# Normalising a key tile ahead of or behind the next tile's evictions, in a fused linear attention and expert kernel

## The chip, the cores and the metric

The kernel runs on one core of a Trainium2 chip. The core has five engines that matter here, each with its own queue of instructions: PE (TensorE, matrix products, with PEld for its weight loads), DVE (VectorE), ACT (ScalarE), POOL (GpSimd) and SP (SyncE, which issues DMAs). The metric is the device time of one execution in microseconds (us). Before the change it is 776.78 us, the median of three runs from 776.26 to 778.11.

## The reference

For 2048 tokens of width 448 a gate mixes two results, `g * a + (1 - g) * b`. `a` is a linear attention with 16 heads of 28 columns, `b` a mixture of 8 experts of which every token uses two. The part that matters here is the feature map of the keys and the state that is summed from it:

```python
pk = jnp.einsum("bhsd,hdf->bhsf", k, w_phi)
phi_k = jnp.concatenate([_softmax(pk, axis=-1), _softmax(-pk, axis=-1)], axis=-1)
kv = jnp.einsum("bhsf,bhsd->bhfd", phi_k, v)
z  = jnp.einsum("bhsf->bhf", phi_k)
num = jnp.einsum("bhqf,bhfd->bhqd", phi_q, kv)
den = jnp.einsum("bhqf,bhf->bhq", phi_q, z)[..., None] + 1e-6
```

The experts of each token come from its two highest logits `xf @ w_gate`, with a softmax over the two as their weights:

```python
topk_idx = jnp.argsort(-logits, axis=-1)[:, :K]
gates = _softmax(topk_val, axis=-1)
for e in range(E):
    w = (gates * (topk_idx == e)).sum(-1, keepdims=True)
    out = out + w * (_silu(xf @ w1[e]) @ w2[e])
```

## The kernel before

The 2048 tokens are cut into 16 tiles of 128 rows (`NT`). Every product is made of three parts, since each operand is split into a rounded part and a rest. The program has three stages: a pass over the key tiles, which sums the state of the attention (about 21 to 111 us of the profile), a pass over the query tiles (to about 215 us), and the experts (the rest).

The pass over the key tiles is the loop at L689. Step t does the following:

- `advance(STEPS[t])` (L692) takes the next piece of `route`, a generator with the routing of 8 tiles: small DVE instructions on 128x64 or 128x8 elements (L436 to L492). `STEPS` gives one piece to each of the steps 9 to 14 and none to step 15.
- `lower` (L694), in steps 10 to 12, takes the maxima of a query tile on DVE (L603) and subtracts them on POOL (L608).
- `norm(t - 1)` (L696) normalises the predecessor's features `ek[t - 1]`: DVE sums them by head and sign (L632) and takes the reciprocals (L633, into `sk`), and POOL multiplies 128x896 features by them (L634). In step 15 it stands behind `key(t)` (L701).
- `key(t)` (L699): 11 matmuls make `pk` in a bank of PSUM (L149); DVE takes each head's maximum and minimum (L625, twice) and evicts the two differences into `ek[t]` in SBUF (L626, L627).
- Behind them come a value tile or a query tile's products on PE (L664), ACT's exponential of `ek[t]` in place (L714), and `store` (L720), which issues indirect DMAs with routing records from POOL (L497).
- `state(t)` (L639) adds a normalised tile to the state on PE (L643). From step 8 on it is called in pairs: step 10 sums tiles 7 and 8, step 12 tiles 9 and 10, step 14 tiles 11 and 12, each pair behind the products of its step. Tiles 13, 14 and 15 follow after the loop (L757, L758, L762), between products of the first query tiles and transposes of `flip` (L745).

The order of the instructions on PE, ACT and DVE is the order in which they are written (`manual_schedule`, L352), and POOL's large instructions and its stores are tied to each other by `in_turn`. `pk` has two banks, so the products of tile t wait until DVE has evicted tile t - 2.

Of the kernel before, what the change touches and what calls it, by code (L numbers as in the profile page):

```python
# [25 lines left out]
NT = S // P  # L26
# [57 lines left out]
KLATE = 7  # L84
# [10 lines left out]
def gated_mix(ctx: ExitStack, tc: tile.TileContext, xt, xq, wk, wq, wv, wphi, wo, w12, out):  # L95
# [39 lines left out]
    def in_turn(i, kind=None):  # L135
        if runs["on"]:
            if kind is None or kind != runs["kind"]:
                runs.update(before=runs["last"], last=[], kind=kind)
            for o in runs["before"]:
                follow(i, o)  # L140
            runs["last"].append(i)
        return i
# [52 lines left out]
    def load_in_turn(dst, src):  # L195
        i = nc.sync.dma_start(dst, src)
        if loads:
            follow(i, loads[-1])
        loads.append(i)
        return i  # L200
# [50 lines left out]
    for what in LANDING:  # L251
        t = int(what[1])
# [52 lines left out]
    def xsplits(t):  # L305
        xsplit(XH[t], XL[t], xr[t], nc.gpsimd if t in XLP else nc.vector)
        if t + 3 < NT:
            xload(t + 3)
# [4 lines left out]
    def fold(n, c):  # L313
        f = [bank("O", f"wf{n}{c}{a}")[:, 0:D].rearrange("p (c g f) -> p c g f", c=2, g=4) for a in range(2)]
        for i in range(2):
            for g in range(4):
                for a, k in enumerate(half):
                    for b in half:
                        nc.tensor.matmul(f[a][b, i, g], raw[n][k, c + i, g * P + b.start:g * P + b.stop], bd[k, g],
                                         start=True, stop=True)  # L320
        for a in range(2):
            split(*(w[n][:, c:c + 2].rearrange("p c (g a f) -> p a c g f", g=4, a=2)[:, a] for w in (WH, WL)), f[a])
# [19 lines left out]
    def value(t):  # L342
        pv = bank("O", f"pv{t}")
        mm3(pv[:, 0:VG], kpairs(XH[t], XL[t], WH["v"], WL["v"]))
        value_out(t, pv)
# [149 lines left out]
    def store(n, behind=()):  # L495
        for at, what in stores[:n]:
            i = in_turn(nc.gpsimd.indirect_dma_start(  # L497
                out=tabd[:, :], out_offset=bass.IndirectOffsetOnAxis(ap=at, axis=0), in_=what, in_offset=None), "slots")
            after(i, [*filled, *behind])
            for o in sc:  # L500
                tc.declare_no_dep(i.ins, o.ins, reason="slots of their own")
            sc.append(i)
        del stores[:n]
# [91 lines left out]
    def signs(e, src):  # L595
        e4 = signed(e)
        nc.scalar.activation(e4[:, :, 0], src, AF.Copy)
        nc.scalar.activation(e4[:, :, 1], src, AF.Copy, scale=-1.0)
# [12 lines left out]
    def lower(e, n, pool):  # L611
        drop(e, tops(e, n, pool))


    def key(t):
        pk = bank("A", f"pk{t}")
        mm3(pk[:, 0:D], (kpairs if t else as_they_come)(XH[t], XL[t], WH["k"], WL["k"]))
        p = by_head(pk[:, 0:D])

        ek[t] = (pb.tile([P, 4, 512], F32, tag="wraw", name=f"ek{t}").rearrange("p c n -> p (c n)")[:, 0:2 * D]  # L620
                 if t >= KLATE and t % 2 else pb.tile([P, 2 * D], F32, tag="e", name=f"ek{t}", bufs=KLAG + 1))
        e4 = halves(ek[t])
        mx = [pb.tile([P, H], F32, tag=f"mk{i}", name=f"mk{i}_{t}") for i in range(2)]
        for m, op in zip(mx, (ALU.max, ALU.min)):
            nc.vector.tensor_reduce(out=m, in_=p, axis=AX.X, op=op)  # L625
        nc.vector.tensor_tensor(out=e4[:, :, 0], in0=p, in1=mx[0].unsqueeze(2).to_broadcast(b16), op=ALU.subtract)  # L626
        nc.vector.tensor_tensor(out=e4[:, :, 1], in0=mx[1].unsqueeze(2).to_broadcast(b16), in1=p, op=ALU.subtract)  # L627

    def norm(t):
        e = ek[t]  # L630
        s_ = pb.tile([P, 2 * H], F32, tag="s", name=f"sk{t}")
        nc.vector.tensor_reduce(out=s_, in_=by_head(e), axis=AX.X, op=ALU.add)  # L632
        nc.vector.reciprocal(s_, s_)  # L633
        in_turn(nc.gpsimd.tensor_tensor(out=by_head(e), in0=by_head(e), in1=s_.unsqueeze(2).to_broadcast([P, 2 * H, DH]),  # L634
                                        op=ALU.mult))
# [3 lines left out]
    def state(t):  # L639
        for g in range(4):  # L640
            for i in range(4):
                h = 8 * (g // 2) + 2 * i + g % 2
                nc.tensor.matmul(kvp[32 * i:32 * i + 32, g * 56:(g + 1) * 56], vbuf[t % len(vbuf)][:, h, :],  # L643
                                 ek[t][:, h * 56:(h + 1) * 56], start=t == 0 and g == 0, stop=t == NT - 1,
                                 skip_group_check=True)
# [3 lines left out]
    def advance(n):  # L649
        for _ in range(n):  # L650
            if routes and next(routes[0], 0) == 0:
                del routes[0]
# [4 lines left out]
    def ask(t, b=None, some=(0, 11)):  # L657
        if some[0] == 0:
            b = bank("A", f"pq{t}") if b is None else b
            pq[t] = by_head(b[:, 0:D])  # L660
            EQ[t] = ebuf[t % QBUFS]
        for k, (x, w) in enumerate(kpairs(XH[t], XL[t], WH["q"], WL["q"])):
            if some[0] <= k < some[1]:
                nc.tensor.matmul(pq[t].rearrange("p h d -> p (h d)"), x, w, start=k == 0, stop=k == 10)  # L664

    def raise_(t):
        nc.scalar.activation(EQ[t][:, :, 0:56], EQ[t][:, :, 0:56], AF.Exp)
# [21 lines left out]
    for t in range(NT):  # L689
        u = t + VAHEAD  # L690
        q = ASKS.get(t)
        advance(STEPS[t])  # L692
        if t - QWAIT in ASKS and ASKS[t - QWAIT] < QEARLY:
            lower(EQ[ASKS[t - QWAIT]], f"q{ASKS[t - QWAIT]}", pr)  # L694
        if 1 <= t < NT - 1:
            norm(t - 1)  # L696
        for v in SPLITS.get(t, ()):
            xsplits(v)
        key(t)  # L699
        if t == NT - 1:  # L700
            norm(t - 1)  # L701
        if u < NT:
            value(u)
        if q is not None:
            ask(q, early[:, q % 2 * 512:q % 2 * 512 + 512])
            signs(EQ[q], pq[q])
        if t in (2, 4):
            fold("q", t - 2)
        if 1 <= t < 5:
            c = t - 1  # L710
            nc.scalar.activation(WH["o"][:, c], raw["o"][:, c], AF.Copy)
            in_turn(nc.gpsimd.tensor_tensor(out=WL["o"][:, c], in0=raw["o"][:, c], in1=WH["o"][:, c].bitcast(F32),
                                            op=ALU.subtract))
        nc.scalar.activation(ek[t], ek[t], AF.Exp)  # L714
        if t - QWAIT in ASKS and ASKS[t - QWAIT] < QEARLY:
            raise_(ASKS[t - QWAIT])
        if t == 8:
            for r in range((NOUT - S) // P):
                rows_done.append(load_in_turn(out[S + r * P:S + (r + 1) * P, :], zero[:, 0:D]))
        store(KSTORES.get(t, 2))  # L720
        if KLAG <= t <= KLATE + 1:
            state(t - KLAG)
        elif t > KLATE and (t - KLATE) % 2:
            state(t - KLAG - 1)
            state(t - KLAG)
        if u + 1 in GROUPS:
            routes.append(route(GROUPS.index(u + 1) - 1))
# [796 lines left out]
```

## Time and profile before

| | us |
|---|---|
| median of three runs | 776.78 |
| lowest, highest | 776.26, 778.11 |
| profiled execution | 776.68 |
| its span, first to last instruction | 775.0 |
| outside the span | 1.68 |
| PE busy in the span | 764.5 |
| DVE busy in the span | 470.1 |
| POOL busy in the span | 343.9 |

The page shows one execution; its times count from the start of the span. An engine's busy time is the sum of its instructions. In a timeline each row gives an instruction's start, its duration, engine, line, operation, and what it writes and reads; a bracket at the end gives the idle time just before it and what ended that. A row with "x2" merges two of a kind. Instructions of DVE and ACT overlap a little with the next, so that a row can start before the end of the one above it.

### The profile page before, as it was taken

The numbers are of one execution on the slowest core, as the hardware profiler recorded it, in microseconds if no ns is written. First come the engines' busy times: TensorE is split into PE (matmuls) and PEld (weight loads), VectorE is DVE, ScalarE is ACT, GpSimd is POOL, SyncE is SP. The second block draws the span as 40 slices with busy tenths as digits, with TensorE's granted clock in tenths as the row PEclk, the third lists the DMA queues.
The fourth block names the chain that finished last, engine by engine and source line by source line (L and its number), as shares of the span: only waits on it lengthen the run. The fifth ranks groups of instructions, "written<-read, shape, count | busy, mean of one in ns | idle before, by whom it ended". The sixth has DMA issues, their size and how long they took to land. (4 is left out here: it accounts for less than half of the span.)

```text
span 775.0 us, 21224 instructions
## 1 busy us (share of the span) xinstructions
PE 764.5 (99%) x8890; PEld 714.3 (92%) x8890; DVE 470.1 (61%) x954; ACT 304.9 (39%) x522; POOL 343.9 (44%) x321
## 2 busy tenths in 40 slices
PE   9999999999999999999999999999999999999996
PEld 7888888888899999998999899999998999999996
DVE  4698978768766755565457345554654555465442
ACT  5543456567433333333334323332432333243220
POOL 4667877886224305521472337054234405423102
PEclk9999999999999999999999999999999999999999
DMA  8420000156344327433643454363345336434502
GB/s 277 131 88 1 2 2 27 39 114 209 114 155 123 128 102 154 134 106 95 147 142 124 90 149 151 111 157 132 127 114 157 128 111 160 137 125 112 168 2 48
DMA packets 42759, 88.95 MB, mean 115 GB/s; under 512 B 11438, under 2 KB 23126, under 8 KB 42660
## 3 DMA queue, kind: packets, MB, share of 16 engines
q1 hardware_dynamic: 32324, 70.24, 27.5%
q0 software_dynamic: 10192, 17.08, 11.3%
q8 instruction: 71, 1.16, 0.6%
q10 hardware_dynamic: 144, 0.23, 0.1%
q14 instruction: 28, 0.23, 0.1%
HBM read 73.53 MB, written 14.00 MB: 113 GB/s over the span
## 5 line engine op out<-in xcount | busy, mean ns | idle before, releaser
L1130 PE MATMUL acc<-w2h,hx 64*128 64x448 f32 (+3 forms) x1756 | 293.4, 362 | 0.0
L1071 PE MATMUL hp<-xgh,w1h 64*128 64x272 f32 (+4 forms) x1078 | 218.3, 331 | 0.9 <-SPq L1048 0.8
L1071 PE MATMUL hp<-xgh,w1l 64*128 64x272 f32 (+4 forms) x1078 | 217.7, 331 | 0.0
L1071 PE MATMUL hp<-xgl,w1h 64*128 64x272 f32 (+4 forms) x1078 | 217.5, 330 | 0.0
L1130 PEld LDWEIGHTS acc<-w2h,hx 64*128 64x128 f32 (+3 forms) x1756 | 200.1, 182 | 4.9 <-issue 1.0
L1104 DVE CAST hx<-hs 128x504 fp32r<-128x504 f32 (+5 forms) x154 | 55.3, 359 | 231.5 <-ACT hs L1098 231.4
L1130 PE MATMUL acc<-w2l,hx 64*128 64x448 f32 (+4 forms) x892 | 195.1, 362 | 0.0
L1098 ACT ACTIVATE hs<-hp 128x272 f32<-128x272 f32 (+4 forms) x154 | 66.3, 482 | 313.4 <-issue 216.7
L847 POOL DMA_INDIRECT xg<-in_xq_dram,idq x114 | 128.9, 1131 | 131.9 <-PE hp L1071 65.6
L1071 PEld LDWEIGHTS hp<-xgh,w1h 64*128 64x128 f32 x1078 | 145.3, 184 | 5.8 <-SPq L1048 1.2
L1071 PEld LDWEIGHTS hp<-xgl,w1h 64*128 64x128 f32 x1078 | 143.9, 184 | 4.0
L1071 PEld LDWEIGHTS hp<-xgh,w1l 64*128 64x128 f32 x1078 | 143.7, 184 | 3.1
L1023 POOL DMA_INDIRECT out_dram<-y,tabm x30 | 48.6, 1620 | 195.8 <-DVE y L1221 189.1
L1130 PEld LDWEIGHTS acc<-w2l,hx 64*128 64x128 f32 (+4 forms) x892 | 110.6, 182 | 2.2
L1107 DVE TENSOR_TENSOR hx<-hs,hx 128x504 fp32r<-128x504 f32 (+6 forms) x168 | 85.0, 513 | 5.3
L816 DVE TENSOR_TENSOR w1l<-wr,w1h 128x1024 fp32r<-128x1024 f32 x56 | 67.7, 1210 | 2.2 <-ACT w1h L814 2.1
L814 ACT ACTIVATE w1h<-wr 128x1024 fp32r<-128x1024 f32 x56 | 59.3, 1058 | 4.8 <-DMA wr<-in_w_dram 4.8
L816 DVE TENSOR_TENSOR w2l<-wr,w2h 128x896 fp32r<-128x896 f32 x46 | 49.5, 1076 | 0.0
L814 ACT ACTIVATE w2h<-wr 128x896 fp32r<-128x896 f32 x46 | 43.9, 954 | 0.0
L497 POOL DMA_INDIRECT tabd<-rec,slot_i x32 | 31.5, 984 | 10.1 <-issue 8.1
L634 POOL TENSOR_TENSOR ek<-ek,sk 128x896 f32<-128x896 f32 x16 | 27.2, 1700 | 16.8 <-DVE sk L633 10.3
L867 ACT ACTIVATE xgh<-xgt 128x512 fp32r<-128x512 f32 (+4 forms) x30 | 18.1, 605 | 39.5 <-DVE xgt L875 39.5
(242 smaller groups left out, 1004.1 us busy)
## 6 DMA issues: line engine op xcount, KB each, us to landing
wr<-in_w_dram SPq DMA_DIRECT2D x56, 512.0 KB, 3.7
wr<-in_w_dram SPq DMA_DIRECT2D x46, 448.0 KB, 4.3
kept<-in_w_dram SPq DMA_DIRECT2D x10, 448.0 KB, 5.5
out_dram<-aos SPq DMA_DIRECT2D x16, 224.0 KB, 2.6
xr<-in_xt_dram SPq DMA_DIRECT2D x10, 256.0 KB, 4.0
xg<-in_xq_dram,idq POOLq DMA_INDIRECT x114, 3.3
xr<-in_xt_dram SPq DMA_DIRECT2D x6, 192.0 KB, 3.9
out_dram<-zero SPq DMA_DIRECT2D x5, 224.0 KB
```

What stands on the lines that cost most here:

```text
L497: i = in_turn(nc.gpsimd.indirect_dma_start(out=tabd[:, :], out_offset=bass.IndirectOffsetOnAxis(ap=at, axis=0), in_=what, in_offset=None), ...
L634: in_turn(nc.gpsimd.tensor_tensor(out=by_head(e), in0=by_head(e), in1=s_.unsqueeze(2).to_broadcast([P, 2 * H, DH]), op=ALU.mult))
L814: nc.scalar.activation(h, raws[s][layer - 1], AF.Copy)
L816: nc.vector.tensor_tensor(out=l, in0=raws[s][layer - 1], in1=h.bitcast(F32), op=ALU.subtract)
L847: i = nc.gpsimd.indirect_dma_start(out=t[:, b], out_offset=None, in_=xq, in_offset=bass.IndirectOffsetOnAxis(ap=idq[:, e, 4 * c + b:4 * c ...
L867: nc.scalar.activation(xh, src, AF.Copy)
L1023: return nc.gpsimd.indirect_dma_start(out=out, out_offset=bass.IndirectOffsetOnAxis(ap=idx_ap, axis=0), in_=y, in_offset=None, compute_op= ...
L1071: meet(("first", i), a, lambda: nc.tensor.matmul(o[i], l, r, start=n == 0, stop=n == len(rounds) - 1), n == 0)
L1098: nc.scalar.activation(hs[:, tsl], hp, AF.Silu)
L1104: nc.vector.tensor_copy(h[:, tsl], hs[:, tsl])
L1107: nc.vector.tensor_tensor(out=h[:, a + o:b + o], in0=hs[:, a:b], in1=h[:, a:b].bitcast(F32), op=ALU.subtract)
L1130: meet((e, c), a, lambda: nc.tensor.matmul(acc[e][c][:l.shape[1], 0:D], l[half[a]], r[half[a]], start=new, stop=ends and c not in of[k + 1 ...
```

## The change

The bound between the two places of `norm(t - 1)` moves from step 15 to step 10. In the steps 10 to 14 the predecessor was normalised ahead of `key(t)`, and is now normalised behind it, as in step 15 before and after. `KLATE` is 7.

```diff
         advance(STEPS[t])
         if t - QWAIT in ASKS and ASKS[t - QWAIT] < QEARLY:
             lower(EQ[ASKS[t - QWAIT]], f"q{ASKS[t - QWAIT]}", pr)
-        if 1 <= t < NT - 1:
+        if 1 <= t < KLATE + 3:
             norm(t - 1)
         for v in SPLITS.get(t, ()):
             xsplits(v)
         key(t)
-        if t == NT - 1:
+        if t >= KLATE + 3:
             norm(t - 1)
         if u < NT:
             value(u)
```

On DVE, from the queue of step 10 into step 11, stood before (`sk` the sums and their reciprocals, `mk` maxima and minima, `pk` the products in PSUM, `mxq` a query tile's maxima, `f`, `sel` and `l` parts of the routing):

```order
L632 TENSOR_REDUCE sk_1179<-ek_1126 128x32
L633 RECIPROCAL sk_1179<-sk_1179 128x32
L625 TENSOR_REDUCE mk_10_1196<-pk_1183 128x16
L625 TENSOR_REDUCE mk_10_1197<-pk_1183 128x16
L626 TENSOR_TENSOR ek_1195<-pk_1183,mk_10_1196 128x16x28
L627 TENSOR_TENSOR ek_1195<-mk_10_1197,pk_1183 128x16x28
L440 TENSOR_REDUCE f_1172<-t_1171 128x8
L441 TENSOR_TENSOR sel_1166<-down,f_1172 128x64
L451 SCALAR_TENSOR_TENSOR l_1168<-sel_1166,L 128x64
L603 TENSOR_REDUCE mxq_1253<-eq_205 128x32
```

and now:

```order
L625 TENSOR_REDUCE mk_10_1192<-pk_1179 128x16
L625 TENSOR_REDUCE mk_10_1193<-pk_1179 128x16
L626 TENSOR_TENSOR ek_1191<-pk_1179,mk_10_1192 128x16x28
L627 TENSOR_TENSOR ek_1191<-mk_10_1193,pk_1179 128x16x28
L632 TENSOR_REDUCE sk_1198<-ek_1126 128x32
L633 RECIPROCAL sk_1198<-sk_1198 128x32
L440 TENSOR_REDUCE f_1172<-t_1171 128x8
L441 TENSOR_TENSOR sel_1166<-down,f_1172 128x64
L451 SCALAR_TENSOR_TENSOR l_1168<-sel_1166,L 128x64
L603 TENSOR_REDUCE mxq_1253<-eq_205 128x32
```

The sum and the reciprocal of tile 9 moved behind the four evictions of tile 10, and so directly ahead of the routing piece of step 11.

Further on, from step 13 into step 14, stood before on DVE (`gt` and `omg` are the gate and one minus the gate, 8 tiles at a time):

```order
L632 TENSOR_REDUCE sk_1379<-ek_1319 128x32
L633 RECIPROCAL sk_1379<-sk_1379 128x32
L625 TENSOR_REDUCE mk_13_1396<-pk_1383 128x16
L625 TENSOR_REDUCE mk_13_1397<-pk_1383 128x16
L626 TENSOR_TENSOR ek_1395<-pk_1383,mk_13_1396 128x16x28
L627 TENSOR_TENSOR ek_1395<-mk_13_1397,pk_1383 128x16x28
L459 TENSOR_SCALAR gt<-gt 128x8
L460 RECIPROCAL gt<-gt 128x8
L461 TENSOR_SCALAR omg_1163<-gt 128x8
```

and now:

```order
L625 TENSOR_REDUCE mk_13_1392<-pk_1379 128x16
L625 TENSOR_REDUCE mk_13_1393<-pk_1379 128x16
L626 TENSOR_TENSOR ek_1391<-pk_1379,mk_13_1392 128x16x28
L627 TENSOR_TENSOR ek_1391<-mk_13_1393,pk_1379 128x16x28
L632 TENSOR_REDUCE sk_1398<-ek_1315 128x32
L633 RECIPROCAL sk_1398<-sk_1398 128x32
L459 TENSOR_SCALAR gt<-gt 128x8
L460 RECIPROCAL gt<-gt 128x8
L461 TENSOR_SCALAR omg_1163<-gt 128x8
```

Here too the pair moved from ahead of the evictions to the place directly ahead of the routing piece. No instruction is added or removed; on PE, ACT, POOL and SP the sequence of operations is the same as before.

## Rows read from the trace of the kernel before

**Rows 1.** The page's part 1: busy time, share of the span and number of instructions of each engine.

```profile
PE 764.5 (99%) x8890; PEld 714.3 (92%) x8890; DVE 470.1 (61%) x954; ACT 304.9 (39%) x522; POOL 343.9 (44%) x321
```

**Rows 2.** Busy time by stretch, one answer each for 74 to 112 us and for 112 us to the end: the length of the stretch, then busy us (and instructions) of PE, PEld, DVE, ACT, POOL, the granted TensorE clock, the DMA share, GB/s.

```profile
74.00:112.00 38.00, 37.34 (x455) 32.86 (x454) 32.84 (x67) 18.66 (x33) 30.56 (x24) 1.00 0.02 2
...
112.00:775.00 663.00, 654.80 (x7660) 619.90 (x7658) 382.88 (x771) 251.04 (x412) 268.00 (x221) 1.00 0.42 120
```

**Rows 3.** Who waited for whom, PE over the whole span: us in total, times, longest.

```profile
PE warm L246 <- DVE blank L244: 1.1, 1, 1.1
PE hp L1071 <- SPq L1048: 0.8, 1, 0.8
PE et L745 <- ACT et L746: 0.7, 1, 0.7
PE n L936 <- DVE w L952: 0.6, 2, 0.3
PE ot L969 <- POOL om L957: 0.5, 1, 0.5
```

**Rows 4.** Timeline of all engines around the start of step 11.

```profile
81.98 1.71 POOL L634 TENSOR_TENSOR ek<-ek,sk 128x896 f32<-128x896 f32 x1
...
83.04 0.21 DVE L440 TENSOR_REDUCE f<-t 128x8 f32<-128x64 f32 x1
...
83.29 0.50 DVE L441 TENSOR_TENSOR sel<-down,f 128x64 f32<-128x64 f32 x1
...
83.82 0.29 DVE L451 SCALAR_TENSOR_TENSOR l<-sel,L 128x64 f32<-128x64 f32 x1
```

**Rows 5.** Timeline of DVE from step 12 to the start of step 15.

```profile
88.47 0.22 DVE L436 TENSOR_REDUCE m<-l 128x8 f32<-128x64 f32 x1
88.72 0.25 DVE L437 TENSOR_TENSOR t<-l,m 128x64 f32<-128x64 f32 x1
89.00 0.23 DVE L438 TENSOR_TENSOR t<-t,down 128x64 f32<-128x64 f32 x1
...
91.25 0.35 DVE L633 RECIPROCAL sk<-sk 128x32 f32<-128x32 f32 x1
91.52 1.08 DVE L625 TENSOR_REDUCE mk<-pk 128x16 f32<-128x448 f32 x2
...
93.58 0.21 DVE L440 TENSOR_REDUCE f<-t 128x8 f32<-128x64 f32 x1
...
94.04 0.06 DVE L454 MEMSET selb<- 128x4 uint32 x1
...
94.75 1.09 DVE L632 TENSOR_REDUCE sk<-ek 128x32 f32<-128x896 f32 x1 [0.33 <-ACT ek L714]
95.88 0.35 DVE L633 RECIPROCAL sk<-sk 128x32 f32<-128x32 f32 x1
...
98.21 0.17 DVE L459 TENSOR_SCALAR gt<-gt 128x8 f32<-128x8 f32 x1
...
98.64 0.17 DVE L461 TENSOR_SCALAR omg<-gt 128x8 f32<-128x8 f32 x1
99.44 1.09 DVE L632 TENSOR_REDUCE sk<-ek 128x32 f32<-128x896 f32 x1 [0.62 <-ACT ek L714]
...
102.89 1.15 DVE L625 TENSOR_REDUCE mk<-pk 128x16 f32<-128x448 f32 x2
...
106.13 0.35 DVE L633 RECIPROCAL sk<-sk 128x32 f32<-128x32 f32 x1
```

**Rows 6.** Timeline of POOL from step 13 to the end of the key tiles: the multiplications of tiles 12, 13, and (merged) 14 and 15, and two stores.

```profile
96.39 1.70 POOL L634 TENSOR_TENSOR ek<-ek,sk 128x896 f32<-128x896 f32 x1 [1.55 <-DVE sk L633]
...
101.09 1.70 POOL L634 TENSOR_TENSOR ek<-ek,sk 128x896 f32<-128x896 f32 x1 [0.57 <-DVE sk L633]
102.94 1.00 POOL L497 DMA_INDIRECT tabd<-rec,slot_i  x1 [0.16 <-issue]
104.25 0.98 POOL L497 DMA_INDIRECT tabd<-rec,slot_i  x1 [0.30 <-issue]
106.64 3.36 POOL L634 TENSOR_TENSOR ek<-ek,sk 128x896 f32<-128x896 f32 x2 [1.41 <-DVE kvs L750]
```

**Rows 7.** Timeline of DVE at three earlier or later places where the routing's instructions ran while POOL worked.

```profile
34.95 1.07 DVE L438 TENSOR_TENSOR t<-t,down 128x64 f32<-128x64 f32 x1
...
53.63 0.83 DVE L461 TENSOR_SCALAR omg<-gt 128x8 f32<-128x8 f32 x1
...
122.31 1.11 DVE L490 TENSOR_TENSOR s<-sel,slot 128x64 f32<-128x64 f32 x1
...
123.71 0.23 DVE L490 TENSOR_TENSOR s<-sel,slot 128x64 f32<-128x64 f32 x1
```

**Rows 8.** Timeline of POOL at the same three places.

```profile
34.79 1.15 POOL L712 TENSOR_TENSOR WLo<-wraw_o,WHo 128x448 fp32r<-128x448 f32 x1
...
53.29 1.14 POOL L712 TENSOR_TENSOR WLo<-wraw_o,WHo 128x448 fp32r<-128x448 f32 x1
...
121.64 1.70 POOL L608 TENSOR_TENSOR eq<-eq,mxq 128x896 f32<-128x896 f32 x1
```

**Rows 9.** Timeline of the weight loads at the two ends of the state's sum that the change reaches: the state of tiles 11 and 12, and of tile 15.

```profile
98.93 0.94 PEld L643 LDWEIGHTS kv<-ek,v 128*32 128x32 f32 x64 [0.31 <-issue]
...
110.05 0.45 PEld L643 LDWEIGHTS kv<-ek,v 128*32 128x32 f32 x32 [0.32 <-POOL ek L634]
```

## The prediction, written before the result was known

> **What bounds the kernel now.** I read the page's busy times first. PE is busy for 764.5 us of 775.0 [rows 1], so any time PE loses is lost for good, and what another engine saves is worth nothing unless PE waited for it. Next come the busy times by stretch, since the change lies in one of them: from 74 to 112 us PE is busy for 37.34 of 38.00 us, but DVE for 32.84 and POOL for 30.56 [rows 2]. In this stretch the two are close behind PE, unlike in the rest. Then PE's waits: none is over 1.1 us, and between 74 and 112 us there is one of 0.7 us, at a transpose [rows 3]. The one edge through which the normalisation ends the stretch is the state of tile 15: its first weight load, at 110.05 us, was released by POOL's multiplication [rows 9], which ends at 106.64 + 3.36 = 110.00 [rows 6]. So the key pass ends on the chain from DVE to POOL to PE, and it has no room there.
>
> Last, the timelines of DVE and POOL side by side, for who runs at the same time as whom. This decides the forecast. A routing instruction on DVE that reads two operands from SBUF takes about 0.25 us (L437 and L438 in step 12) [rows 5]. While a POOL multiplication or subtraction runs, the same kind takes until that has ended: L438 from 34.95 to 36.02, beside a POOL instruction that ends at 34.79 + 1.15 = 35.94; L461 to 54.46 beside one to 54.43; L490 to 123.42, 1.11 us, beside POOL's L608 to 123.34, and 0.23 us right after with POOL free [rows 7, 8]. Once the normalising multiplication does it too: L441 takes 0.50 us and ends at 83.79, 0.10 behind POOL's L634 [rows 4]. The evictions, with one operand in PSUM, are not held: those of tile 13 take 2.06 us from 96.15 to 98.21, like those of tile 12 [rows 5], with a multiplication beside them from 96.39 to 98.09 [rows 6].
>
> The Trainium skill has this as a rule: in "SBUF — State Buffer", section "Who interferes with whom", a VectorE instruction with two SBUF inputs contends with a GpSimd instruction that reads SBUF, and the port they share goes to one of them for a whole instruction. The trace agrees, with the 1.07, 0.83 and 1.11 us above. By the rule alone the change would be slower as well, by as many blocks.
>
> **The change, part by part.** Nothing is added or removed. In steps 10 to 14 the sum and the reciprocal go behind the evictions, which take 2.06 us from start to start (91.52 to 93.58) [rows 5]. Take r, the start of the reciprocal. POOL's multiplication starts at r + 0.51 (95.88 to 96.39) [rows 5, 6] and runs for 1.70, to r + 2.21; DVE's next instruction starts at r + 0.27 (91.25 to 91.52).
>
> Before, that next work was the evictions, with one operand in PSUM, and the routing piece followed at r + 0.27 + 2.06 = r + 2.33, when the multiplication was over. That is a fit to a tenth of a microsecond. After, the routing piece of the next step starts at r + 0.27, and the whole multiplication stands against it; the piece's blocked instruction ends near r + 2.30.
>
> - Step 11: r is 82.77, since step 11 still starts at 83.04. L441 then ends at 85.07 and L451 starts at 85.10 where it started at 83.82 [rows 4]: 1.28 us.
> - Step 12: L438 started 0.53 us into the step (89.00 - 88.47) and now starts at r + 2.33, which is 2.06 into it: 1.53 us.
> - Step 13: L454, behind L441, started 0.46 into the step (94.04 - 93.58) and now 1.98: 1.52 us.
> - Step 14: L461 ended 0.60 into the step (98.64 + 0.17 - 98.21) and now ends with the multiplication, 1.97 into it: 1.37 us.
>
> The sum is 5.70 us on DVE. Who comes first in steps 11 to 13 is open, as L441 or L437 would start at r + 0.52 and POOL at r + 0.51. It matters little: if DVE wins, POOL starts 0.26 later, and the next two-operand instruction of the piece (L451, L438, L455) is held instead. Only if POOL let the whole piece pass would a step cost nothing. So a block is bounded by 0 and 1.8 us, and I take the values above, since every overlap in rows 4, 7 and 8 shows DVE held.
>
> What goes away: DVE's two waits for the exponential, 0.33 us in step 13 and 0.62 in step 14 [rows 5], because a tile's sum now comes one key tile later. DVE is then 5.70 - 0.95 = 4.75 us late at the evictions of tile 15, which start at 102.89 + 4.75 = 107.64.
>
> On POOL a moved normalisation also moves its multiplication, past no other instruction, but later against the clock. Tile 13's reciprocal now stands directly ahead of tile 15's evictions, r = 107.37, so its multiplication starts at 107.88. The two stores of step 14 lie behind it in POOL's queue: 1.85 us from the multiplication's start to the first, 1.31 to the second, 1.0 for that one [rows 6]. So tile 14 starts at 112.04. Its reciprocal, at 106.13 + 4.75 = 110.88, would have allowed 111.39: the queue adds 0.65. Tiles 14 and 15 take 3.36 together, to 115.40, and the state of tile 15 starts at 115.45 where it started at 110.05: 5.4 us.
>
> On PE the wait shows up first at the state of tile 12, in step 14. Step 14 starts at 98.21 + 1.28 + 1.53 + 1.52 - 0.33 = 102.21, so tile 12 is multiplied from 102.45 to 104.15. PE would be there near 100 us (the pair started at 98.93 [rows 9], and the products of tile 14 lose about 0.7 us before that, because the evictions of tile 12 free their bank later). PE then stands for some 4 us. This is part of the 5.4 and not on top of it: behind it the products of tile 15 end near 107, before DVE asks for them at 107.64, and PE waits again at the states of tiles 14 and 15. The 0.7 us wait at the transpose goes into the same delay.
>
> Behind 112 us nothing gives it back: PE is busy for 654.80 of 663.00 us there [rows 2], and its named waits add up to 0.8 + 0.6 + 0.5 = 1.9 us [rows 3]. I take none of it as absorbed; at most it is those 1.9, which would leave 780.3 us.
>
> The profiled execution took 776.68 us, 1.68 more than its span; 776.68 + 5.4 = 782.1. It lies 0.10 under the median of the runs, so the forecast for the median is 782.2 us.
>
> **The rivals.**
>
> *No block, not slower.* POOL waits for the short routing instructions instead of holding them. Then only order is left. The multiplications come about 1.9 us later in steps 13 and 14 (behind 2.06 us of evictions, less the waits that vanish); tile 12's would end at about 100.0, and its state, at 99.4 in PE's order, would wait 0.6 us. The 0.95 us of vanished waits repay most of this at tile 15. The sum comes to about +0.1 us: 776.9 us. It decides if DVE's routing pieces keep their 0.25 us. Against it stand all the overlaps in the rows.
>
> *Half of it.* In steps 11 and 12, where the start is a race of 0.01 us, the routing piece passes ahead of POOL, and only steps 13 and 14 pay: 1.52 + 1.37 = 2.89, less the 0.95 that vanishes, plus 0.65 of the queue, about +2.6 us: 779.4 us for the median. If step 13 is spared too, it is 1.52 less: 777.9. It decides if POOL's start slips by the length of the piece's two instructions, some 0.5 us. For it speaks that the race is so close, against it that no row shows DVE passing.
>
> *The clock as well.* The granted clock is 1.00 in both stretches [rows 2], the higher level of 2.4 GHz, and PE never waited over 1.1 us [rows 3]. Four microseconds of standing at the state of tile 12 have no precedent in this trace. If the clock fell to its lower level there, the products of tile 15, 11 matmuls in some 2.3 us, would take about 2.3 more, and DVE would start tile 15's evictions at about 109.4 in place of 107.64. With the 0.65 us of the store queue hidden by this, and the transposes behind also slower, it adds some 1.3 us: 783.5 us. The Trainium skill's "TensorE: Matmul & The Clock Gate", Part 1, says that the default state is throttled and that activity releases it, so that a long enough pause costs the higher level. No row here shows such a fall, nor a pause as long.
>
> **How the numbers follow.** Forecast 0.62, half of it 0.16, the clock too 0.13, no block 0.06, something that I don't see, to the faster side, 0.03. The range of 779.2 to 784.2 takes in the forecast with its blocks up to 0.3 us longer each, most of the half case and the clock case. A measurement of this kernel can tell about 0.3% from no change, 2.3 us, so slower means over 779.1. The forecast, the clock case and 0.10 of the half case lie above: 0.85. The rest of the half case, the case without a block and most of the unseen lie within: 0.13. Faster by 2.3 us has no mechanism, since all of PE's waits in the stretch add up to 1 us: 0.02.
>
> **What would show it.** DVE's L441 or L451, L437 or L438, L441 or L455, and L461 between 83 and 104 us take 1.3 to 1.8 us in place of 0.17 to 0.50, each ending about 0.1 us behind a POOL L634; the waits of L632 for ACT in steps 13 and 14 are gone; PE waits some 4 us for POOL's `ek` at L643 near 100 us; the state of tile 15 starts near 115.5 us; DVE's busy time grows by about 5.5 us and PE's hardly. If the routing rows keep their length, the reason is wrong; if they grow and the end does not, something downstream had room that I didn't see.

## The result and the profile after

The changed kernel takes 781.50 us, the median of 14 runs (779.91 to 785.13); the kernel before takes 776.27 in its 14 runs (775.14 to 778.49). The ratio is 1.0067, with a 95% interval of 1.0053 to 1.0080: 5.2 us slower. The prediction said 782.2, in a range of 779.2 to 784.2.

The profiled execution of the changed kernel took 783.25 us, with a span of 781.5; the kernel before had a span of 775.0. The page's part 1 answers to [rows 1]:

```profile
PE 768.4 (98%) x8890; PEld 717.3 (92%) x8890; DVE 475.4 (61%) x954; ACT 304.9 (39%) x522; POOL 343.5 (44%) x321
```

The counts of instructions are the same. DVE is busy 5.3 us longer, POOL hardly differs, and PE is busy 3.9 us longer with the same work: 1.1 of it ahead of step 10, where this execution ran a little later, and 2.8 from there to the state of tile 15, at a lower clock (the end of this section).

The timeline of DVE from step 11 to step 14 answers to [rows 4, 5]. Its times are not comparable at once: in this execution step 10 began 0.83 us later (its L436 at 78.78 us; 77.95 before), and 0.83 is taken off below wherever two profiles are compared.

```profile
83.66 0.35 DVE L633 RECIPROCAL sk<-sk 128x32 f32<-128x32 f32 x1
...
84.13 0.23 DVE L441 TENSOR_TENSOR sel<-down,f 128x64 f32<-128x64 f32 x1
84.39 1.61 DVE L451 SCALAR_TENSOR_TENSOR l<-sel,L 128x64 f32<-128x64 f32 x1
...
90.61 0.23 DVE L437 TENSOR_TENSOR t<-l,m 128x64 f32<-128x64 f32 x1
90.87 1.61 DVE L438 TENSOR_TENSOR t<-t,down 128x64 f32<-128x64 f32 x1
...
95.52 1.07 DVE L632 TENSOR_REDUCE sk<-ek 128x32 f32<-128x896 f32 x1
...
97.09 0.23 DVE L441 TENSOR_TENSOR sel<-down,f 128x64 f32<-128x64 f32 x1
97.27 0.06 DVE L454 MEMSET selb<- 128x4 uint32 x1
97.35 1.61 DVE L455 TENSOR_TENSOR selb<-sel,sel 128x64 bf16<-128x64 f32 x1
...
102.84 1.58 DVE L461 TENSOR_SCALAR omg<-gt 128x8 f32<-128x8 f32 x1
104.33 1.14 DVE L625 TENSOR_REDUCE mk<-pk 128x16 f32<-128x448 f32 x2
...
107.57 0.35 DVE L633 RECIPROCAL sk<-sk 128x32 f32<-128x32 f32 x1
109.86 0.62 DVE L625 TENSOR_REDUCE mk<-pk 128x16 f32<-128x448 f32 x1 [1.94 <-PE pk L149]
```

The timeline of POOL over the same steps and to the end of the key tiles, which answers to [rows 6]:

```profile
84.16 1.75 POOL L634 TENSOR_TENSOR ek<-ek,sk 128x896 f32<-128x896 f32 x1 [1.30 <-DVE f L440]
...
90.67 1.73 POOL L634 TENSOR_TENSOR ek<-ek,sk 128x896 f32<-128x896 f32 x1 [1.85 <-DVE m L436]
...
97.15 1.73 POOL L634 TENSOR_TENSOR ek<-ek,sk 128x896 f32<-128x896 f32 x1 [1.85 <-DVE f L440]
...
102.70 1.69 POOL L634 TENSOR_TENSOR ek<-ek,sk 128x896 f32<-128x896 f32 x1 [2.67 <-DVE gt L459]
```

In each of the steps 11 to 14 one routing instruction takes 1.6 us in place of about 0.2 to 0.3, and ends 0.03 to 0.09 us behind POOL's multiplication: L451 at 84.39 + 1.61 = 86.00, POOL at 84.16 + 1.75 = 85.91. In steps 11 to 13 the first two-operand instruction (L441, L437, L441) starts 0.03 to 0.06 us ahead of POOL and passes in 0.23; the next one is held. In step 14 the held instruction (L461, which reads one tensor and not two) starts 0.14 us behind POOL. The sums of steps 13 and 14 (L632 at 95.52, and at 101.09) no longer wait for ACT.

Then PE. Of its waits over the whole span (us in total, times, longest), which answer to [rows 3], one is new in size:

```profile
PE kv L643 <- POOL ek L634: 3.6, 2, 3.5
```

Its place is in PE's timeline around the state of tile 12; behind it stand two rows of the weight loads at the end of the key tiles, which answer to [rows 9]:

```profile
100.39 0.60 PE L643 MATMUL kv<-ek,v 128*32 128x56 f32 x32
104.44 0.98 PE L643 MATMUL kv<-ek,v 128*32 128x56 f32 x32 [3.45 <-POOL ek L634]
105.35 0.74 PE L149 MATMUL pk<-WHk,XH 128*128 128x448 f32 x1
105.89 0.57 PE L149 MATMUL pk<-WLk,XH 128*128 128x448 f32 x1
106.26 0.57 PE L149 MATMUL pk<-WHk,XH 128*128 128x448 f32 x1
```

```profile
115.27 0.85 PEld L643 LDWEIGHTS kv<-ek,v 128*32 128x32 f32 x64 [0.31 <-issue]
117.02 0.45 PEld L643 LDWEIGHTS kv<-ek,v 128*32 128x32 f32 x32 [0.32 <-POOL ek L634]
```

PE stands for 3.45 us where tile 12 is not yet multiplied. Behind that the products of tile 15 follow each other every 0.37 us, while those of the query tile just ahead of the pause (L664, 98.05 to 99.68 us) came every 0.2. The busy times by stretch, with the granted clock in the third column from the right, show that too:

```profile
100.00:104.00 4.00, 0.99 (x35) 0.53 (x33) 3.90 (x8) 1.91 (x4) 1.33 (x2) 0.86 0.01 0
104.00:110.00 6.00, 5.56 (x47) 4.83 (x48) 4.03 (x8) 0.95 (x1) 4.10 (x5) 0.53 0.02 3
```

At 0.53 the clock is near its lower level of 1.2 GHz in the second stretch, so the same matmuls take longer and count as busy. The 0.86 of the first stretch says that it fell inside the pause, before the work began again at 104.44. DVE, which is ready for tile 15's evictions at 107.57 + 0.27 = 107.84, waits 1.94 us for them. The state of tile 15 starts at 117.02 - 0.83 = 116.19, 6.14 us later than at 110.05 before.

### The profile page after: what moved, and what is told of

Same layout as the page of the kernel before. It is cut to its first block, busy times and chain, and to the rows that moved or that the text cites. A ratio compares the mean times of both kernels' runs of the same rounds, so it can differ in the third digit from the quotient of the medians.

```text
span 781.5 us, 21224 instructions
## 1 busy us (share of the span) xinstructions
PE 768.4 (98%) x8890; PEld 717.3 (92%) x8890; DVE 475.4 (61%) x954; ACT 304.9 (39%) x522; POOL 343.5 (44%) x321
## 5 line engine op out<-in xcount | busy, mean ns | idle before, releaser
L497 POOL DMA_INDIRECT tabd<-rec,slot_i x32 | 31.5, 984 | 10.0 <-issue 8.0
```

The source lines that it names most:

```text
L497: i = in_turn(nc.gpsimd.indirect_dma_start(out=tabd[:, :], out_offset=bass.IndirectOffsetOnAxis(ap=at, axis=0), in_=what, in_offset=None), ...
```

## The experiments

The theory: routing instructions on DVE (L451, L438 and L455 with two operands in SBUF, and L461 with one) are held by POOL's multiplication, which the moved normalisation places beside them; the time is the number of such blocks times about 1.3 us, and the store queue adds some. The rival: the order alone costs it, since each multiplication now comes behind the evictions and PE waits for it, whatever DVE does. The runs were made in several series, on different chips. Each difference below is taken to the kernel before in the same series, and "the lateness of tile 15" is the start of its state's first weight load less the start of L436 in step 10, compared with the 32.10 us in the one profile of the kernel before.

| kernel | held routing instructions | lateness of tile 15, us | median, against before, us |
|---|---|---|---|
| changed | 4 | 6.14 | +5.2 |
| changed, routing out of the way | 0 | 1.28 | +0.7 |
| before, routing out of the way | 0 | 1.67 | +1.3 |
| normalised behind from step 12 | 2 | 2.94 | +2.1 |
| normalised behind from step 14 | 0 | 0.04 | 0.0 |
| changed, PE kept busy (first) | 4 | 5.63 | +6.3 |
| changed, PE kept busy (second) | 4 | 4.82 | +5.9 |
| the same without step 14's stores | 4 | 4.05 | +6.1 |
| changed, multiplication in halves (first) | 5, of about half the length | 2.53 | +2.7 |
| changed, second profile | 4 | 5.35 | +4.0 |
| changed, multiplication in halves (again) | 5, of about half the length | 2.53 | +3.1 |
| changed, third profile | 4 | 5.15 | +5.0 |

Not counted are the 0.50 us of L441 in step 11, which the kernel before has too and which stay in the two kernels that are normalised behind from step 12 and 14.

**The routing taken out of the way.** The five pieces of steps 10 to 14 all run in step 10, in the changed kernel and in the kernel before.

```diff
-STEPS = (0, 0, 1, 1, 2, 2, 2, 2, 2, 1, 1, 1, 1, 1, 1, 0)
+STEPS = (0, 0, 1, 1, 2, 2, 2, 2, 2, 1, 5, 0, 0, 0, 0, 0)
```

Changed kernel:

> The changed kernel with all five routing pieces of steps 10 to 14 taken in step 10, ahead of the moved normalisations, so that none stands behind a reciprocal. Held routing (the theory): no two-operand routing instruction runs beside a normalising multiplication; L438, L441, L451, L455 and L461 keep 0.1 to 0.3 us, the four stretches of 1.6 us are gone, and the time falls from 781.5 to within 0.5 to 1.5 us of before, some 777 to 778 us (the five pieces at once delay the evictions of tiles 10 to 12 by up to 3 us, which costs PE a little at the states of tiles 10 and 12). Order alone (the rival: the multiplication comes late because it stands behind the evictions, whatever DVE does beside it): still about +4 to +5 us, 780.5 us or more, with PE's wait of over 3 us at the state of tile 12.

Kernel before:

> The kernel before with the same five routing pieces taken in step 10: the other half of the pair. Held routing: the same cost of the regrouping as in the changed kernel, about +0.5 to +1.5 us, so that the two kernels of the pair lie within 1 us of each other. Order alone: this one stays near 776.3 to 777.5, and the pair lies 4 us or more apart, as the two kernels without the regrouping do.

Measured: 776.93 us (ratio 1.0012, 1.0002 to 1.0023) and 777.57 us (1.0015, 1.0006 to 1.0024). In the changed kernel with the routing in step 10, L455 takes 0.23 and L461 0.17 us, from DVE's timeline of it:

```profile
81.05 0.23 DVE L455 TENSOR_TENSOR selb<-sel,sel 128x64 bf16<-128x64 f32 x1
...
81.71 0.17 DVE L461 TENSOR_SCALAR omg<-gt 128x8 f32<-128x8 f32 x1
```

Its multiplications still stand behind the evictions in all five steps, and it is no slower than the kernel before with the same routing; PE waits at most 0.8 us for a multiplication there, in place of 3.45. So the order of the normalisation by itself costs nothing that these runs can tell; beside the routing pieces it costs 5.2 us. The rival falls.

**Half of the change.** The bound is put two and four steps later, so that two blocks and none are left.

```diff
-        if 1 <= t < KLATE + 3:
+        if 1 <= t < KLATE + 5:
...
-        if t >= KLATE + 3:
+        if t >= KLATE + 5:
```

From step 12 on:

> Normalised behind the evictions from step 12 on in place of step 10. Held routing: two stretched routing instructions (in steps 13 and 14) in place of four, L441 and L451 of step 11 and L437 and L438 of step 12 as in before; the sum gives +2.4 us, some 778.7 us, with PE's wait at the state of tile 12 near 1.5 to 2 us and the clock at its higher level. Order alone: the state of tile 12 is what PE waits for, and tile 12 is normalised behind the evictions here as well, so the same time as the changed kernel, 780.5 us or more.

From step 14 on (KLATE + 7):

> Normalised behind the evictions only from step 14 on. A move without any routing piece behind it: step 15 has none. Held routing: no stretched routing instruction beyond the 0.5 us of L441 that the kernel before has, the 0.62 us wait of step 14 for ACT gone, PE without a wait at the state of tile 12; the time within 0.5 us of before, on either side. Order alone: a multiplication behind the evictions costs its 2 us wherever it is, so +1 us or more, at the states of tiles 13 to 15.

Measured: 778.35 us for the first (ratio 1.0027, 1.0016 to 1.0039) and 776.09 for the second (0.9997, 0.9986 to 1.0008). DVE's timeline of the first has two held instructions, and in step 11 the short hold of L441 that the kernel before has too:

```profile
83.67 0.49 DVE L441 TENSOR_TENSOR sel<-down,f 128x64 f32<-128x64 f32 x1
...
94.50 1.61 DVE L455 TENSOR_TENSOR selb<-sel,sel 128x64 bf16<-128x64 f32 x1
...
99.99 1.58 DVE L461 TENSOR_SCALAR omg<-gt 128x8 f32<-128x8 f32 x1
```

The second has none beyond that of L441, though step 14's normalisation is moved. None, two and four held instructions cost 0.0, 2.1 and 5.2 us. One thing missed: the clock was expected to hold with two blocks, as PE waits only 1.68 us. It fell here too, in the timeline and the windows of PE:

```profile
101.59 0.60 PE L643 MATMUL kv<-ek,v 128*32 128x56 f32 x32 [1.68 <-POOL ek L634]
102.12 0.68 PE L149 MATMUL pk<-WHk,XH 128*128 128x448 f32 x1
102.59 0.58 PE L149 MATMUL pk<-WLk,XH 128*128 128x448 f32 x1
```

```profile
98.00:101.60 3.60, 1.92 (x41) 1.40 (x40) 3.50 (x7) 1.99 (x4) 1.69 (x1) 1.00 0.00 0
101.60:104.50 2.90, 2.90 (x39) 2.59 (x40) 2.90 (x5) 0.79 (x1) 1.97 (x2) 0.61 0.01 0
```

**The clock.** Extra matmuls, whose result is overwritten, fill the pause at the state of tile 12. The first try puts 14 of them into one half of a query tile's pair of banks, between the two states of step 14:

```diff
+            if t == 14:
+                for i in range(14):
+                    nc.tensor.matmul(early[:, 512:960], XH[0][:, 0], WH["q"][:, 0], start=True, stop=True)
```

> The changed kernel with 14 more matmuls between the states of tiles 11 and 12, on loaded operands and into a half bank that nothing reads any more: about 2.9 us of PE work in the 3.5 us that PE stands there. Clock theory (the pause costs the higher clock, and that part of the time is the clock's): the products of tile 15 keep a pitch of about 0.2 us, DVE no longer waits 1.9 us for them, the granted clock is 1.00 between 100 and 110 us, and the median falls by 1 to 1.5 us to about 780.2, with a smaller spread than the 779.9 to 785.1 of the changed kernel. Rival (the slow products come from something else, or their price is hidden behind the multiplications): no change of the median, or slower by what the extra matmuls add. Four routing instructions of 1.6 us in either case.

Measured: 782.52 us (1.0082, 1.0066 to 1.0098). It missed: the extra matmuls themselves waited for ACT (L598), which was still reading those banks, and ended only at 105.28 us, some 2 us after POOL's multiplication, so they lengthened the pause of the real work:

```profile
102.22 3.13 PE L727 MATMUL early<-WHq,XH 128*128 128x448 f32 x14 [2.22 <-ACT eq L598]
105.28 0.60 PE L643 MATMUL kv<-ek,v 128*32 128x56 f32 x32
...
106.12 0.37 PE L149 MATMUL pk<-WLk,XH 128*128 128x448 f32 x1
106.33 0.36 PE L149 MATMUL pk<-WHk,XH 128*128 128x448 f32 x1
```

It says nothing on the price of the clock; it shows that after a pause of 2.22 us the products kept their pitch of 0.2 us. The second try writes 13 matmuls into tile 15's own bank, which is overwritten by its products:

```diff
+    made = {}
+
     def key(t):
-        pk = bank("A", f"pk{t}")
+        pk = made.pop(t, None)
+        pk = bank("A", f"pk{t}") if pk is None else pk
...
+            if t == 14:
+                made[15] = bank("A", "pk15")
+                for i in range(13):
+                    nc.tensor.matmul(made[15][:, 0:D], XH[15][:, 0], WH["k"][:, 0], start=True, stop=True)
```

> The changed kernel with 13 more matmuls between the states of tiles 11 and 12, this time into the bank of tile 15's products, which is free once tile 13 is evicted (their sums are overwritten by the products that follow): 2.7 us of PE work that fits into the 3.5 us pause without lengthening it. Clock theory: tile 15's products keep a pitch of 0.2 us at a granted clock of 1.00, DVE waits under 0.5 us for them in place of 1.9, and the median falls from 781.5 to 780.0 to 780.7, the level of those runs of the changed kernel whose mean clock is 0.996 or more (median 780.6). Rival, that the clock's part is hidden behind the store queue and the multiplications: the median stays at 781.5 within 0.3. The four routing instructions of 1.6 us stay in either case.

And with the stores of step 14 taken to the end of the key tiles besides:

```diff
-TSTORES = 1
-KSTORES = {10: 1, 11: 1, 12: 1, 15: 0}
+TSTORES = 3
+KSTORES = {10: 1, 11: 1, 12: 1, 14: 0, 15: 0}
```

> The same, and the two stores of step 14 issued behind the loop, with the one that is there, in place of between the multiplications of tiles 13 and 14. Queue theory (the prediction's 0.65 us): tile 14's multiplication follows its reciprocal by 0.2 us in place of waiting for the second store, the state of tile 15 comes 0.4 to 0.9 us earlier, and the median is 0.4 to 0.9 us under after_busy2. Rival (the reciprocals of tiles 14 and 15 are as late as the stores, or the two stores cost as much behind): within 0.2 us of after_busy2.

Measured: 781.99 us (1.0079, 1.0055 to 1.0103) and 782.16 us (1.0068, 1.0049 to 1.0087). In the key pass both did what the theory said. PE's timeline of the second try has no wait over 0.32 us and no slow products there, and DVE has no wait for them:

```profile
100.27 2.86 PE L731 MATMUL pk<-WHk,XH 128*128 128x448 f32 x13 [0.32 <-DVE ek L630]
103.41 0.60 PE L646 MATMUL kv<-ek,v 128*32 128x56 f32 x32 [0.28 <-POOL ek L637]
...
104.25 0.36 PE L149 MATMUL pk<-WLk,XH 128*128 128x448 f32 x1
104.44 0.37 PE L149 MATMUL pk<-WHk,XH 128*128 128x448 f32 x1
```

The lateness of tile 15 is 4.82 us in place of 6.14, and 4.05 without the stores. So in the key pass the clock was worth 1.3 us of the first profile of the changed kernel, and the store queue 0.77. The time did not follow: 780.0 to 780.7 was expected of the second try, and without the stores another 0.4 to 0.9 less, where the median was 0.17 more. In the variant without the stores the 0.77 is lost at once. The three stores, now together behind the key tiles, keep POOL from clearing `z`, and DVE waits for that, in DVE's timeline of the variant:

```profile
120.03 0.19 DVE L954 TENSOR_TENSOR z<-n,r 128x32 f32<-128x32 f32 x1 [1.20 <-POOL z L934]
```

That is the rival of its expectation, that the stores cost as much behind. What the second try won is lost near 186 us in its profile, at a wait of DVE and then of PE; the two timelines of the second try there:

```profile
184.41 0.71 DVE L882 STREAM_TRANSPOSE xgt<-xg 128x512 f32<-128x512 f32 x1 [1.71 <-DMA xg<-by_row]
```

```profile
187.62 1.16 PE L943 MATMUL n<-B,et 64*64 64x60 f32 x64 [1.53 <-DVE w L959]
```

The rows gathered for the experts arrive too late for the transpose by 1.71 us, and by 1.45 us in the variant without the stores; the kernel before waits 0.44 us for them. Three profiles of the changed kernel itself wait 0, 0.74 and 0.88 us, the last of them in DVE's timeline:

```profile
184.01 0.71 DVE L875 STREAM_TRANSPOSE xgt<-xg 128x512 f32<-128x512 f32 x1 [0.88 <-DMA xg<-by_row]
```

So this wait changes from one execution to the next, and one profile of each variant doesn't show that the extra matmuls lengthened it. The chain to these rows begins with the routing's table, which is stored (L497) and read back before the rows are gathered: from the start of the last store to the start of the first gather it is 5.70 us in the kernel before and 5.71 in the first profile of the changed one, 6.36 and 5.83 in these two variants; from there to the transpose it is 15.00 us in the kernel before, 15.65 and 15.90 in the variants. Why is open, and with it what the clock is worth in the time of the whole kernel.

**The multiplication in halves.** If POOL holds DVE for the length of one instruction, two shorter ones should hold it for half as long. Tiles 9 to 12, which stand beside the routing, are multiplied in two instructions of 16 heads by sign.

```diff
-        in_turn(nc.gpsimd.tensor_tensor(out=by_head(e), in0=by_head(e), in1=s_.unsqueeze(2).to_broadcast([P, 2 * H, DH]),
-                                        op=ALU.mult))
+        for lo, hi in ((0, H), (H, 2 * H)) if KLATE + 2 <= t <= KLATE + 5 else ((0, 2 * H),):
+            in_turn(nc.gpsimd.tensor_tensor(out=by_head(e)[:, lo:hi], in0=by_head(e)[:, lo:hi],
+                                            in1=s_[:, lo:hi].unsqueeze(2).to_broadcast([P, hi - lo, DH]), op=ALU.mult))
```

> The changed kernel with POOL's multiplication of tiles 9 to 12 issued as two halves of 16 heads each (the four that stand against a routing piece); the others stay whole. A half is priced by POOL's 128x448 rows at 1.15 us, so a tile costs POOL some 0.6 us more. Theory of the held instruction, with DVE let in between two POOL instructions: the held routing instruction starts 0.23 us behind POOL and ends about 0.1 behind the first half, so it takes about 1.0 us in place of 1.6; four times 0.55 to 0.6 us less, 2.2 to 2.4, so about 779.3 us (778.5 to 780.3) beside 781.2 to 781.5 of the whole multiplication. Rival A, DVE held until POOL's queue has a pause: the second half follows at once, the held instruction takes about 2.1 us, the kernel becomes some 2 us slower, about 783.5. Rival B, only the lateness of the multiplications counts: each ends 0.6 us later than in the changed kernel, about 782, whatever DVE's rows show.

The changed kernel beside it:

> The changed kernel unchanged, for a second profile and a second set of runs on the same chip as the split. About 781.3 us. The mean granted clock of its runs should again fall into two groups, at and above 0.996 with about 780.6 us and below it with about 782.5. If its profile is of the upper group, the products of tile 15 keep a pitch near 0.2 us and the state of tile 15 comes about 1.3 us earlier than in the first profile; if the pitch is 0.37 us again in a run of the upper group, the groups have another cause than the fall at tile 15.

In this series, on another chip than the other experiments, the kernel before took 795.91 us. The profiles of both kernels here have waits of PE behind 240 us (9.3 us in all in the changed kernel's) that the other series' profiles don't show; the kernel before has no profile of this series, and what caused the waits is open. The split took 798.59 (1.0033, 1.0009 to 1.0058), the changed kernel 799.93 (1.0041, 1.0018 to 1.0064). The times, which spread over 8 to 10 us, tell little; the traces are clear. So both were run once more:

> The split of the multiplication of tiles 9 to 12 into two halves once more, for its time, since the kernel before took 795.9 us instead of 776.3 in the series of the first try, with waits for weights behind 240 us that no other profile here shows. In the first try the four held instructions took 0.85, 0.85, 0.85 and 0.82 us instead of 1.6, and the state of tile 15 came at 112.36 us instead of 115.22 in the changed kernel of that series. Theory of the held instruction: where the kernel before takes about 776.3, this takes 776.3 + 5.2 - 2.9 = 778.6 us (778 to 779.8). If the time of the changed kernel did not come from those blocks, it stays at 781 to 782.

> The changed kernel unchanged, beside the split in the same series: about 781.3 us where the kernel before takes 776.3, with two groups of runs by the mean granted clock, about 780.6 and 782.5. In both profiles so far the pause at the state of tile 12 was 3.45 us and the products of tile 15 had a pitch of 0.37 us behind it; a third profile with a clock of 0.996 or more and a pitch of 0.2 would tie the groups to this place, a pitch of 0.37 there would part them from it.

Measured, beside 776.40 us of the kernel before: 779.48 us for the split (1.0052, 1.0034 to 1.0071) and 781.40 for the changed kernel (1.0065, 1.0052 to 1.0078). The split's DVE and POOL in steps 11 and 13:

```profile
83.29 0.23 DVE L441 TENSOR_TENSOR sel<-down,f 128x64 f32<-128x64 f32 x1
83.55 0.85 DVE L451 SCALAR_TENSOR_TENSOR l<-sel,L 128x64 f32<-128x64 f32 x1
...
95.00 0.85 DVE L455 TENSOR_TENSOR selb<-sel,sel 128x64 bf16<-128x64 f32 x1
95.78 0.92 DVE L456 TENSOR_TENSOR m<-m,m 128x8 f32<-128x8 f32 x1
```

```profile
83.32 1.90 POOL L635 TENSOR_TENSOR ek<-ek,sk 128x448 f32<-128x448 f32 x2 [1.29 <-DVE f L440]
...
94.80 1.88 POOL L635 TENSOR_TENSOR ek<-ek,sk 128x448 f32<-128x448 f32 x2 [0.95 <-DVE f L440]
```

DVE is let in between the two halves, although they stand back to back in POOL's queue: L451 takes 0.85 in place of 1.61. In step 13 a second instruction (L456) meets the second half and is held for 0.92, which nobody had reckoned with. Tile 15 is 2.53 us late in place of the third profile's 5.15, and the median is 1.9 us under the changed one's. With six and five runs the two intervals overlap, so it is the rows that carry this, and the same 2.53 us in both profiles of the split. Nothing but POOL's grain was changed, so the hold lasts as long as one POOL instruction. A half costs some 0.95 us, not the 1.15 assumed, which is why the hold came out shorter than the 1.0 expected. The Trainium skill says in "SBUF — State Buffer", section "Who interferes with whom", that the port pair which VectorE and GpSimd share is locked for a whole instruction; the 0.85 against 1.61 us agree.

The second and third profiles of the changed kernel answer the question on the clock only in part. The pause was 3.45 and 3.43 us, and the clock fell in both, but later than in the first, after the work had begun again: in the third, the first products still came at a pitch of 0.2 us before it rose to 0.37, and the clock was 0.72 from 104 to 110 us (0.53 in the first). DVE waited 0.95 us for them in place of 1.94. In the first series 7 of its 14 runs had a mean clock of 0.996 or more and a median of 780.58 us, the other 7 had 782.49; here its five runs all have 0.996 and 780.81 to 782.25 us, so the two groups did not show again, and a higher mean clock does not mean that there was no fall at tile 15.

## Why the prediction was right, and where its terms were off

**The blocks.** The mechanism is as predicted: one held instruction in each of steps 11 to 14, each ending about 0.1 us behind POOL. Their sum was put at 5.70 us. From the starts of the pieces (rows L633 plus 0.27: 83.93, 90.41, 96.89, 102.46 and 107.84) the steps last 6.48, 6.48, 5.57 and 5.38 us; before they lasted 5.43, 5.11, 4.63 and 4.68 [rows 4, 5]. The differences are 1.05, 1.37, 0.94 and 0.70, to which the vanished waits of 0.33 and 0.62 in the last two are added back: 1.05, 1.37, 1.27 and 1.32, 5.01 us. The predicted 1.28, 1.53, 1.52 and 1.37 were each a little too long. In steps 11 to 13 the rows say why: DVE won the race, so it was the second two-operand instruction that was held, and the first, which the sum had held, was already done. L603 starts 1.99 us into steps 11 and 12, where the prediction's rows put it at about 2.3 and 2.2.

**The race.** "It matters little" was right: DVE came 0.03 to 0.06 us ahead of POOL in steps 11 to 13, its first instruction passed in 0.23, and the next was held. The rival that let whole pieces pass fell, since only one two-operand instruction passed in each.

**One reading was wrong.** The prediction counts L461 among the instructions with two operands in SBUF. It is a `TENSOR_SCALAR` that reads `gt` alone. It was held all the same, for 0.83 us at 53.63 before and for 1.58 here, so the price of step 14 stands, but its 0.83 is no example of the rule for two inputs, and a list by two operands alone would have missed it.

**The vanished waits.** The 0.95 us went, as the rows without a bracket at L632 show. DVE was ready for tile 15 at 107.84 - 0.83 = 107.01, 4.12 us later than at 102.89; the prediction had 4.75.

**PE's wait at tile 12.** Predicted some 4 us near 100, measured 3.45 from 100.99 to 104.44. It is shorter mainly by the same overestimate of the blocks: POOL's multiplication starts at 102.70 - 0.83 = 101.87, where 102.45 was predicted.

**The store queue.** Predicted 0.65 us at the state of tile 15, measured 0.77 there by the run without those stores (4.82 - 4.05). In the first profile it was hidden behind DVE's wait, as the clock rival had said.

**The clock.** Here the weights were wrong. It had a chance of 0.13, and all three profiles of the changed kernel show it. In the first it is worth 6.14 - 4.82 = 1.3 us in the key pass, the price named in that rival; in the other two 0.5 and 0.3 (5.35 and 5.15 less 4.82). PE's busy time, which was hardly to grow, grew by 3.9 us in the first profile, 2.8 of them in this stretch at the lower clock. So the forecast of +5.4 at tile 15 stands on two errors that nearly cancel: with the clock held it is 4.82, 0.6 less than said, because the blocks were 0.7 us too long, and the clock gave back 0.3 to 1.3. That the median came within 0.7 us of the forecast is in part luck.

**What comes behind.** The prediction let nothing be absorbed. In the first profile the span grew by 6.5 us, from 6.14 of lateness at tile 15 and 0.83 from ahead of step 10: 0.5 was given back behind the key pass, 0.3 of it at the rows gathered for the experts, for which the kernel before waits 0.44 us and this execution not at all. The prediction didn't look there; the runs show it as a wait that ends differently from one execution to the next.

## What to carry to other kernels

Before moving a POOL instruction, list which DVE instructions will stand beside it in its new place: those with two operands in SBUF, and such as L461 here, which reads one. Each time, the one that meets it costs the rest of POOL's instruction, not its own 0.2 us. Where both must overlap, shorter POOL instructions let DVE in between, and put evictions from PSUM there rather than small SBUF work. A gain of a microsecond at the end of a stage is not yet a gain of the kernel; find the next wait that will end last.

## What the runs showed that was not expected

The length of the pause does not decide by itself whether the clock falls. It fell after 1.68 us of waiting with the bound at step 12, and after 3.45 us in the changed kernel, inside the pause in one profile and some 1.2 us after the work had begun again in another (104.72 against 103.48 us). It held after 2.22 us in the first try to keep PE busy, and in the split, where PE waited 1.78 and 0.49 us:

```profile
101.35 0.40 PE L644 MATMUL kv<-ek,v 128*32 128x56 f32 x16 [1.78 <-POOL ek L635]
102.25 0.41 PE L644 MATMUL kv<-ek,v 128*32 128x56 f32 x16 [0.49 <-POOL ek L635]
...
102.89 0.36 PE L149 MATMUL pk<-WLk,XH 128*128 128x448 f32 x1
103.09 0.37 PE L149 MATMUL pk<-WHk,XH 128*128 128x448 f32 x1
```

The Trainium skill's "TensorE: Matmul & The Clock Gate", Part 1, says that activity releases the throttle; the profiles agree in that each fall in the key pass followed a pause of PE. What tells the cases with a fall from those without stays open.

An instruction that reads 128x8 elements is held as long as one of 128x64 (L461 1.58 us beside a whole multiplication, L456 0.92 beside a half), so the smallest routing instruction pays as much as the others.
